# A radix-4 rewrite of the spectral layers of a four-layer mixer, with the layer norms regrouped

## The chip, the cores and the metric

The kernel runs on one core of one Trainium2 chip. The metric is the device time of one execution in microseconds; the kernel before takes 1835.26 us, the median of 4 runs.

## The reference, cut to what matters

The activations x are 2048 rows (S) of 512 columns (D). Two layer types alternate, A, B, A, B, each behind a layer norm without weights and added back to x. A is a spectral filter, a 2-D real FFT, a pointwise complex product with W, and the inverse; B is attention with 32 heads of 16 that share one key and one value head.

```python
def _A_ref(x, w_r, w_i):
    X = jnp.fft.rfft2(x.astype(jnp.float32), axes=(-2, -1))
    X = X * (w_r + 1j * w_i)
    return jnp.fft.irfft2(X, s=(S, D), axes=(-2, -1)).astype(jnp.bfloat16)
...
x = x + _A_ref(_layernorm(x), A_w_r, A_w_i)
x = x + _B_ref(_layernorm(x), B_wq, B_wk, B_wv, B_wo)
x = x + _A_ref(_layernorm(x), A_w_r, A_w_i)
x = x + _B_ref(_layernorm(x), B_wq, B_wk, B_wv, B_wo)
```

## The kernel before, in words

x stays in SBUF as `x_sb[p, r, t, d]`: row 512r + 4p + t, so 16 tiles of 128x512, named by r and t. `xn_sb` holds the normalised tiles in the same form.

**A spectral layer** (`spectral_layer`, `fft_layer`) has four stages, and every matmul in it has 128 rows of contraction.
- Stage A: all tiles are transposed on TensorE (L140), copied out (L146, L152, L154), and multiplied with the table PH of cosines and sines over D (L169); the result, a packed half of 256 real and 256 imaginary columns, is kept twice, as `Ppk` and with its halves swapped and one negated as `Psw` (L171 to L173).
- Stage B: for each t and each m (128 of the 512 frequencies k1), 8 matmuls over r with cosine and sine tables form a 512-point transform along S (L182, L184). ScalarE and VectorE turn the result by the twiddle factors, again into a plain and a swapped copy (L196 to L203). The four t are then combined by butterflies for k2 as matmuls with plus or minus identity (L220), each result of 128x512 is evacuated three times (L222 to L224), multiplied with W in 10 VectorE instructions (L228 to L236) and transformed back over k2 by identity matmuls and twiddles (L252 to L262).
- Stage C: the inverse 512-point transform along S (L277, 16 groups of 8 matmuls), its evacuation `AT` (L279), the inverse over D (L282 to L285) and the addition to x on VectorE (L297).
- The epilogue of each tile is the next layer's norm (`layernorm_tile`): statistics on VectorE (L108, L110), the square root on ScalarE (L112), reciprocal and a bias on VectorE (L113, L115), and the normalisation alternately on ScalarE (L121) and GpSimd (L118).

**An attention layer** starts with stage D: transposes of `xn_sb`, K and the first Q chunk, and V (L140, L342, L326, L355). Then `AttnLoop` writes its order out by hand, step by step: per step TensorE forms scores of two heads for ScalarE's exponential (L389, L500) and of one head for VectorE's (L504); VectorE and GpSimd make shifted copies of the latter (L462, L468); then come the products with V (L402). Every 11th step has no VectorE head and takes a piece from a list: a Q chunk (L326) or an output projection of a tile (`project`: L449, L451). In the first attention layer each projected tile goes on to the next spectral layer's norm (`layernorm_pool`): statistics on VectorE (L93, L95) and four GpSimd instructions (L97 to L102). After 22 steps `evacuate` copies the sums of 4 heads out (L411), and a chain over DRAM divides them. The last 4 projections of a layer come after its last step, when that chain has ended.

The rest of the program, the spectral layers and stage D among it, is put in order by a scheduler; on each engine that order then holds.

## Time and profile before

| | us |
|---|---|
| median of 4 runs (1834.03 to 1835.76) | 1835.26 |
| the profiled execution | 1834.03 |
| its span in the trace | 1831.5 |
| first spectral layer, stages A to C (from the start) | 172.1 |
| stage D and first attention loop with its division chain | 172.1 to 927.3 |
| last projections and second spectral layer | 927.3 to 1081.0 |
| stage D and second attention layer | 1081.0 to 1831.5 |

The 2.5 us between the execution's time and its span lie around the traced span. In the rows below a time is the start or duration of an instruction on the given engine; PE is TensorE's matmuls, DVE VectorE, ACT ScalarE, POOL GpSimd. The bracket at the end of a timeline row says how long the engine was idle ahead of it and what released it. In the rows of groups, the last numbers are busy time, mean duration in ns, and idle time ahead of the group with its releasers. Instructions on one engine overlap a little, so that starts lie closer than durations; a matmul's duration holds the time until its result has left the array.

### The profile page before, as it was taken

The numbers are of one execution on the slowest core, as the hardware profiler recorded it, in microseconds if no ns is written. First come the engines' busy times: TensorE is split into PE (matmuls) and PEld (weight loads), VectorE is DVE, ScalarE is ACT, GpSimd is POOL, SyncE is SP. The second block draws the span as 40 slices with busy tenths as digits, with TensorE's granted clock in tenths as the row PEclk, the third lists the DMA queues.
The fourth block names the chain that finished last, engine by engine and source line by source line (L and its number), as shares of the span: only waits on it lengthen the run. The fifth ranks groups of instructions, "written<-read, shape, count | busy, mean of one in ns | idle before, by whom it ended". The sixth has DMA issues, their size and how long they took to land.

```text
span 1831.5 us, 36065 instructions
## 1 busy us (share of the span) xinstructions
PE 1633.8 (89%) x13760; PEld 508.3 (28%) x13760; DVE 1567.6 (86%) x2919; ACT 1530.1 (84%) x1850; POOL 733.1 (40%) x744
## 2 busy tenths in 40 slices
PE   5878999998999899989868889999999999999995
PEld 2323322222222222222233342222222222222221
DVE  5776699999999999999848757999999999999995
ACT  6444699998999899999844447999999999999994
POOL 2001244456445644564410012444444454454443
PEclk9979899999999999999988898999999999999998
DMA  5000000000000000000000000000000000000000
GB/s 178 1 1 1 1 15 15 15 15 15 15 15 15 15 15 20 16 15 15 15 8 1 1 1 1 15 15 17 22 24 15 15 21 21 15 16 24 23 15 27
DMA packets 38733, 32.43 MB, mean 18 GB/s; under 512 B 21264, under 2 KB 28576, under 8 KB 38560
## 3 DMA queue, kind: packets, MB, share of 16 engines
q1 hardware_dynamic: 37600, 27.89, 5.1%
q8 instruction: 107, 1.75, 0.4%
q0 software_dynamic: 960, 2.25, 0.4%
q14 instruction: 66, 0.54, 0.1%
HBM read 24.88 MB, written 2.62 MB: 15 GB/s over the span
## 4 chain that ended last, share of the span: by engine, by line
PE 53%; DVE 30%; ACT 10%; issue 4%; DMA 2%; POOL 0%; SPq 0%; DVEq 0%; ACTq 0%; POOLq 0%
PE acc_new L402 21%; DVE t L504 13%; PE sd L389 13%; ACT e L500 8%; DVE tj L462 5%; PE sa L389 4%; PE ps L277 3%; DVE odd L437 2%; DVE on_new L434 2%; PE ps L169 2%; PE ps L326 2%; PE ps L449 2%; PE ps L184 2%; PE ps L182 2%; ACT den L411 1%
## 5 line engine op out<-in xcount | busy, mean ns | idle before, releaser
L500 ACT ACTIVATE e<-sa 128x1024 bf16<-128x1024 f32 x1408 | 1323.4, 1105 | 65.3 <-PE sa L389 61.9
L468 POOL TENSOR_SCALAR t<-tj 128x1024 int16<-128x1024 int16 x640 | 672.5, 1051 | 759.1 <-DVE tj L462 442.9
L504 DVE TENSOR_SCALAR t<-sd 128x512 int16<-128x512 f32 x1280 | 830.6, 681 | 76.2 <-PE sd L389 34.4
L389 PE MATMUL sa<-QT,KT 32*128 32x512 bf16 x2816 | 551.4, 385 | 12.1 <-ACT e L500 11.7
L389 PE MATMUL sd<-QT,KT 32*128 32x512 bf16 x1280 | 492.3, 385 | 76.6 <-DVE t L504 75.1
L402 PE MATMUL acc_new<-e,V 128*32 128x512 bf16 x2816 | 557.9, 393 | 1.0 <-ACT e L500 1.0
L462 DVE TENSOR_SCALAR tj<-t 128x2048 int16<-128x2048 int16 x640 | 443.0, 692 | 0.0
L402 PE MATMUL acc_new<-tj,V 128*32 128x512 bf16 x2560 | 386.8, 386 | 2.8 <-DVE tj L462 2.8
L402 PE MATMUL acc_new<-t,V 128*32 128x512 bf16 x2560 | 388.1, 387 | 1.0 <-POOL t L468 1.0
L389 PEld LDWEIGHTS <-KT 32*128 32x128 bf16 x4096 | 195.3, 91 | 690.5 <-issue 689.5
L402 PEld LDWEIGHTS <-V 128*32 128x32 bf16 x7936 | 159.3, 94 | 331.5 <-issue 331.1
L118 POOL TENSOR_SCALAR xn_sb<-x_sb,rstd,nb 128x512 bf16<-128x512 bf16 x16 | 12.2, 767 | 280.1 <-DVE mv L110 147.2
L449 PE MATMUL ps<-wo_sb,on_new 128*128 128x512 bf16 x128 | 36.3, 417 | 24.1 <-DMA on_new<-odd 24.1
L140 PE MATMUL ps<-tab_ident,xn_sb 128*128 128x128 bf16 x256 | 23.9, 248 | 33.2 <-ACT xn_sb L121 18.4
L222 ACT CAST Xs<-ps 128x512 bf16<-128x512 f32 x32 | 18.8, 588 | 37.9 <-DVE m L235 37.6
L297 DVE TENSOR_TENSOR x_sb<-ps,x_sb 128x512 bf16<-128x512 f32 x32 | 21.2, 674 | 32.8 <-PE ps L285 32.8
L437 DVE TENSOR_TENSOR odd<-den,rb 128x512 bf16<-128x512 f32 x32 | 37.5, 1173 | 13.0 <-DMA rb<-rd 12.8
L182 PE MATMUL ps<-Ppk,tab_C 128*128 128x512 bf16 x128 | 48.5, 379 | 0.0
L277 PE MATMUL ps<-tab_C,Dpk 128*128 128x512 bf16 x128 | 48.5, 379 | 0.0
L184 PE MATMUL ps<-Psw,tab_S 128*128 128x512 bf16 x128 | 48.5, 379 | 0.0
L112 ACT ACTIVATE rstd<-mv,eps 128x1 f32<-128x1 f32 x48 | 12.9, 288 | 40.8 <-DVE mv L110 38.2
L411 ACT COPY den<-acc_new 128x512 f32<-128x512 f32 x64 | 39.2, 612 | 8.8 <-PE acc_new L402 8.8
(100 smaller groups left out, 1037.3 us busy)
## 6 DMA issues: line engine op xcount, KB each, us to landing
rb<-rd SPq DMA_DIRECT2D x64, 256.0 KB
...
on_new<-odd SPq DMA_DIRECT2D x128, 16.0 KB
...
dq<-den SPq DMA_DIRECT2D x64, 8.0 KB
rd<-dq SPq DMA_DIRECT2D x64, 8.0 KB
...
```

The costliest lines, as they stand in the source:

```text
L182: nc.tensor.matmul(ps, lhsT=C512[:, r, m * P:(m + 1) * P], rhs=Ppk[:, rt, :], start=(k == 0), stop=False)
L184: nc.tensor.matmul(ps, lhsT=S512[:, r, m * P:(m + 1) * P], rhs=Psw[:, rt, :], start=False, stop=(r == R - 1))
L277: nc.tensor.matmul(ps, lhsT=lt, rhs=tab[:, m, :], start=(k == 0), stop=(k == 7))
L389: self.nc.tensor.matmul(out, lhsT=self.KT[32 * i:32 * i + 32, half, kc * P:(kc + 1) * P], rhs=self.QT[32 * i:32 * i + 32, g, qb * 512:(qb ...
L402: self.nc.tensor.matmul(self.acc[key][32 * i:32 * i + 32, :], lhsT=self.V4[:, kc, j, :], rhs=e, start=first, stop=False, skip_group_check= ...
L411: nc.scalar.copy(out=den, in_=self.acc.pop(key))
L437: nc.vector.tensor_tensor(out=odd, in0=den, in1=rb, op=ALU.mult)
L449: nc.tensor.matmul(ps, lhsT=on[:, g, qt * P:(qt + 1) * P], rhs=self.wo_sb[:, g, :], start=(g == 0), stop=(g == 3))
L462: nc.vector.tensor_scalar(out=tj, in0=cyc["t0"], scalar1=float(SH[j]), scalar2=None, op0=ALU.add)
L468: nc.gpsimd.tensor_scalar(out=cyc["t1"][:, h, :], in0=tj[:, h, :], scalar1=1.0, scalar2=float(SH[1] - SH[j]), op0=ALU.mult, op1=ALU.add)
L500: nc.scalar.activation(out=e, in_=sa, func=ACT.Exp, bias=EXP_LN, scale=SCALE)
L504: nc.vector.tensor_scalar(out=self.dcyc[c]["t0"][:, k, :], in0=sd, scalar1=Y_MUL, scalar2=Y_ADD, op0=ALU.mult, op1=ALU.add)
```

## The change

The spectral layer is rewritten; line numbers below are those of the changed kernel where the text says so.
- Over r, the 4-point butterflies now come first, on VectorE, as sums and differences of whole tiles (`ec`, `xc`, changed L159 to L162). Transposes and PH products keep their number (L169, L178), and 4 VectorE instructions and 3 ScalarE copies per t form `Y`.
- What is left of the transform along S has 128 points. Its twiddles are folded into a table `TAB` of 128 x 12288 (3 MB in all, where the dropped cosine and sine tables had 1.5 MB), and the sum over t runs inside one PSUM group: per (j2, k2) four matmuls of 512 columns (L205) and eight of 256 (L207, L209), where the swap of halves is made by writing to the other half of the bank.
- One evacuation per result (L211) in place of three; products with W and the back butterflies in all 18 VectorE instructions per j2 on 512 and 1024 columns (L214 to L226). There are no swapped copies and no twiddle instructions.
- The inverse along S takes 64 matmuls instead of 128 (L250), with windows of `TAB` as the moving operand, and a sum and a difference on VectorE (L255 to L257). x is added by a fifth matmul per output tile, with the identity (L260), and ScalarE writes the sum to `x_sb` (L266). The PSUM pool has 8 buffers instead of 4.
- The norm is one class for all layers: statistics per tile as before, the inverse root on GpSimd for four tiles at once (changed L105, L106), the normalisation on VectorE (L108) once all four r of a t are there. ScalarE's square root is gone. In the attention loop the four normalisations are put off by 4 to 7 steps.
- `x` is loaded in 4 pieces by t, `w_r` and `w_i` in 4 pieces each by j2; the attention loop's `t0` has 3 buffers.

The diff, cut to its core (shared helper functions and the removed bodies are left out):

```diff
@@ host_tables @@
+    tabs["TAB"] = bf(np.stack([np.sin(ang), np.cos(ang), -np.sin(ang), -np.cos(ang), np.sin(ang), np.cos(ang)], axis=3))
@@ layernorm @@
-def layernorm_pool(nc, lnpool, tabs, x_ap, xn_ap):
-def layernorm_tile(nc, lnpool, tabs, x_ap, xn_ap, on_act=True, use_pool=False):
...
+class LayerNorm:
...
+    def add(self, r, t, later=None):
+        nc = self.nc
...
+        stats = self.lnpool.tile([P, 6], F32, tag="ln_stats", bufs=4)
+        nc.vector.bn_stats(stats, self.x_sb[:, r, t, :])
+        nc.vector.bn_aggr(mv[:, r, :], stats)
+        self.n[t] += 1
+        if self.n[t] == R:
+            self.apply(t, self.mv.pop(t), later)
+    def apply(self, t, mv, later=None):
+        nc = self.nc
+        rstd = self.lnpool.tile([P, R], F32, tag="ln_rstd", bufs=3)
+        nc.gpsimd.tensor_tensor(out=rstd, in0=mv[:, :, 1], in1=self.tabs["eps"], op=ALU.add)
+        nc.gpsimd.tensor_tensor(out=rstd, in0=rstd, in1=self.tabs["mhalf"], op=ALU.pow)
+        def one(r):
+            nc.vector.tensor_scalar(out=self.xn_sb[:, r, t, :], in0=self.x_sb[:, r, t, :],
+                                    scalar1=mv[:, r, 0:1], scalar2=rstd[:, r:r + 1],
+                                    op0=ALU.subtract, op1=ALU.mult)
+        for r in range(R):
+            if later is None:
+                one(r)
+            else:
+                later(4 + r, lambda r=r: one(r))
@@ spectral layer @@
-def fft_layer(nc, tabs, work, psum, xT, wr_sb, win_sb, y_cb):
+def spectral_layer(nc, tc, tabs, x_sb, xn_sb, wr_sb, wi_sb, epilogue):
+    TAB, PH, PSC, PSS, ident = tabs["TAB"], tabs["PH"], tabs["PSC"], tabs["PSS"], tabs["ident"]
+    LO = slice(0, 256)
+    HI = slice(256, 512)
+    with tc.tile_pool(name="workA", bufs=2) as work, tc.tile_pool(name="psA", bufs=8, space=bass.MemoryType.PSUM) as psum:
+        Y = work.tile([P, T, 4, 512], BF, tag="big")
+        for t in range(T):
+            ec = work.tile([P, 2, 2, 512], BF, tag="ec")
+            xc = work.tile([P, 2, 512], BF, tag="xc")
+            nc.vector.tensor_tensor(out=ec[:, 0, :, :], in0=xn_sb[:, 0:2, t, :], in1=xn_sb[:, 2:4, t, :], op=ALU.add)
+            nc.vector.tensor_tensor(out=ec[:, 1, :, :], in0=xn_sb[:, 0:2, t, :], in1=xn_sb[:, 2:4, t, :], op=ALU.subtract)
+            nc.vector.tensor_tensor(out=xc[:, 0, :], in0=ec[:, 0, 0, :], in1=ec[:, 0, 1, :], op=ALU.add)
+            nc.vector.tensor_tensor(out=xc[:, 1, :], in0=ec[:, 0, 0, :], in1=ec[:, 0, 1, :], op=ALU.subtract)
+            xT = work.tile([P, 2, 2, NC, P], BF, tag="xTA")
+            banks = []
+            for pair, src in ((1, ec[:, 1, :, :]), (0, xc)):
+                ps = psum.tile([P, 2, NC, P], BF, tag="pa")
+                for q in range(2):
+                    for cc in range(NC):
+                        nc.tensor.transpose(ps[:, q, cc, :], src[:, q, cc * P:(cc + 1) * P], ident)
+                if pair == 0:
+                    nc.scalar.copy(out=xT[:, pair, :, :, :], in_=ps)
+                else:
+                    nc.vector.tensor_copy(out=xT[:, pair, :, :, :], in_=ps)
+            for pair in (1, 0):
+                for q in range(2):
+                    ps = psum.tile([P, 512], F32, tag="pa")
+                    for cc in range(NC):
+                        nc.tensor.matmul(ps, lhsT=xT[:, pair, q, cc, :], rhs=PH[:, cc, :],
+                                         start=(cc == 0), stop=(cc == NC - 1))
+                    banks.append(ps)
+            psC, psD, psP, psM = banks
+            dd = work.tile([P, 512], F32, tag="dd")
+            nc.scalar.copy(out=dd, in_=psD)
+            nc.vector.tensor_tensor(out=Y[:, t, 1, LO], in0=psC[:, LO], in1=dd[:, HI], op=ALU.subtract)
+            nc.vector.tensor_tensor(out=Y[:, t, 1, HI], in0=psC[:, HI], in1=dd[:, LO], op=ALU.add)
+            nc.vector.tensor_tensor(out=Y[:, t, 3, LO], in0=psC[:, LO], in1=dd[:, HI], op=ALU.add)
+            nc.vector.tensor_tensor(out=Y[:, t, 3, HI], in0=psC[:, HI], in1=dd[:, LO], op=ALU.subtract)
+            nc.scalar.copy(out=Y[:, t, 0, :], in_=psP)
+            nc.scalar.copy(out=Y[:, t, 2, :], in_=psM)
+        V = work.tile([P, T, 4, 512], BF, tag="big")
+        for j2 in range(4):
+            Xs = work.tile([P, 4, 512], BF, tag="Xs")
+            mr = work.tile([P, 4, 2, 256], BF, tag="mr")
+            mi = work.tile([P, 4, 2, 256], BF, tag="mi")
+            Z = work.tile([P, 4, 2, 256], BF, tag="Z")
+            ac = work.tile([P, 2, 2, 256], BF, tag="ac")
+            bd = work.tile([P, 2, 2, 256], BF, tag="bd")
+            Xv = Xs.rearrange("p k (h f) -> p k h f", h=2)
+            for q in range(2):
+                for k2 in (q, q + 2):
+                    ps = psum.tile([P, 512], F32, tag="pa")
+                    for t in range(T):
+                        n = (t * k2) % 4
+                        yt = Y[:, t, j2, :]
+                        nc.tensor.matmul(ps, lhsT=TAB[:, t, j2, (COS + n) % 4, :], rhs=yt, start=(t == 0), stop=False,
+                                         skip_group_check=True)
+                        nc.tensor.matmul(ps[:, LO], lhsT=TAB[:, t, j2, (SIN + n + 2) % 4, :], rhs=yt[:, HI],
+                                         start=False, stop=False, skip_group_check=True)
+                        nc.tensor.matmul(ps[:, HI], lhsT=TAB[:, t, j2, (SIN + n) % 4, :], rhs=yt[:, LO],
+                                         start=False, stop=(t == T - 1), skip_group_check=True)
+                    nc.scalar.copy(out=Xs[:, k2, :], in_=ps)
+                ks = slice(q, q + 3, 2)
+                for m_, w_ in ((mr, wr_sb), (mi, wi_sb)):
+                    nc.vector.tensor_tensor(out=m_[:, ks, :, :], in0=Xv[:, ks, :, :],
+                                            in1=w_[:, j2, ks, :].unsqueeze(2).to_broadcast([P, 2, 2, 256]),
+                                            op=ALU.mult)
+                nc.vector.tensor_tensor(out=Z[:, ks, 0, :], in0=mr[:, ks, 0, :], in1=mi[:, ks, 1, :], op=ALU.add)
+                nc.vector.tensor_tensor(out=Z[:, ks, 1, :], in0=mr[:, ks, 1, :], in1=mi[:, ks, 0, :], op=ALU.subtract)
+                nc.vector.tensor_tensor(out=ac[:, q, :, :], in0=Z[:, q, :, :], in1=Z[:, q + 2, :, :], op=ALU.add)
+                nc.vector.tensor_tensor(out=bd[:, q, :, :], in0=Z[:, q, :, :], in1=Z[:, q + 2, :, :], op=ALU.subtract)
+            Vv = V.rearrange("p t j (h f) -> p t j h f", h=2)
+            nc.vector.tensor_tensor(out=Vv[:, 0, j2, :, :], in0=ac[:, 0, :, :], in1=ac[:, 1, :, :], op=ALU.add)
+            nc.vector.tensor_tensor(out=Vv[:, 2, j2, :, :], in0=ac[:, 0, :, :], in1=ac[:, 1, :, :], op=ALU.subtract)
+            for tt, o0, o1 in ((1, ALU.add, ALU.subtract), (3, ALU.subtract, ALU.add)):
+                nc.vector.tensor_tensor(out=Vv[:, tt, j2, 0, :], in0=bd[:, 0, 0, :], in1=bd[:, 1, 1, :], op=o0)
+                nc.vector.tensor_tensor(out=Vv[:, tt, j2, 1, :], in0=bd[:, 0, 1, :], in1=bd[:, 1, 0, :], op=o1)
+        def window(j2, t, part):
+            tb = TAB[:, j2, t, :, :]
+            b0 = COS if part == 0 else SIN
+            if j2 == 2:
+                return tb[:, b0:b0 + 4, :]
+            w2 = tb[:, b0:b0 + 2, :]
+            if j2 == 0:
+                return w2.unsqueeze(1).to_broadcast([P, 2, 2, P])
+            step = {1: 1, 3: 3}[j2]
+            ap = bass.AP(tensor=w2.tensor, offset=w2.offset, ap=[w2.ap[0], [step * P, 2], [1, 2 * P]])
+            return ap
+        for t in range(T):
+            AT = work.tile([P, 2, 2, 512], BF, tag="AT")
+            for b in range(2):
+                banks = []
+                for js in ((0, 2), (1, 3)):
+                    ps = psum.tile([P, 512], F32, tag="pa")
+                    k = 0
+                    for j2 in js:
+                        for part in range(2):
+                            f0 = part * 256 + b * P
+                            nc.tensor.matmul(ps, lhsT=V[:, t, j2, f0:f0 + P], rhs=window(j2, t, part),
+                                             start=(k == 0), stop=(k == 3))
+                            k += 1
+                    banks.append(ps)
+                gh = work.tile([P, 512], F32, tag="dd")
+                nc.scalar.copy(out=gh, in_=banks[1])
+                nc.vector.tensor_tensor(out=AT[:, b, 0, :], in0=banks[0], in1=gh, op=ALU.add)
+                nc.vector.tensor_tensor(out=AT[:, b, 1, :], in0=banks[0], in1=gh, op=ALU.subtract)
+            for r in range(R):
+                ps = psum.tile([P, 512], F32, tag="pa")
+                nc.tensor.matmul(ps, lhsT=ident, rhs=x_sb[:, r, t, :], start=True, stop=False)
+                for b in range(2):
+                    for part, tab in ((0, PSC), (1, PSS)):
+                        f0 = ((r % 2) * 2 + part) * P
+                        nc.tensor.matmul(ps, lhsT=AT[:, b, r // 2, f0:f0 + P], rhs=tab[:, b, :],
+                                         start=False, stop=(b == 1 and part == 1))
+                nc.scalar.copy(out=x_sb[:, r, t, :], in_=ps)
+                epilogue(r, t)
@@ AttnLoop @@
-        self.epilogue(r, t)
+        self.epilogue(r, t, self.at)
...
-                t0 = self.expp.tile([P, 4, 512], I16, tag="t0")
+                t0 = self.expp.tile([P, 4, 512], I16, tag="t0", bufs=3)
```

How the rows stand on an engine, before and after, at three places. First VectorE in the middle of stage B. Before, these are the rows of one product tile (m_752, m_753 and m_759 are scratch buffers, `win_sb` is the negated imaginary part of W):

```order
L228 TENSOR_TENSOR m_752<-Xs,wr_sb 128x256 [waits DVE_49,Activation_49]
L229 TENSOR_TENSOR m_753<-Xs,win_sb 128x256 [waits Activation_49]
L228 TENSOR_TENSOR m_752<-Xs,wr_sb 128x256
L229 TENSOR_TENSOR m_753<-Xs,win_sb 128x256 [waits Activation_49]
L230 TENSOR_TENSOR Zpk<-m_752,m_753 128x512 [waits DVE_49]
```

After, the second half of one j2, with the butterflies that follow it:

```order
L214 TENSOR_TENSOR mr<-Xs,wr_sb 128x2x512 [waits Activation_49]
L214 TENSOR_TENSOR mi<-Xs,wi_sb 128x2x512
L217 TENSOR_TENSOR Z<-mr,mi 128x2x256 [waits DVE_49]
L218 TENSOR_TENSOR Z<-mr,mi 128x2x256
L219 TENSOR_TENSOR ac<-Z 128x512 [waits DVE_49]
L220 TENSOR_TENSOR bd<-Z 128x512
L222 TENSOR_TENSOR V<-ac 128x512 [waits DVE_49]
L223 TENSOR_TENSOR V<-ac 128x512
L225 TENSOR_TENSOR V<-bd 128x256 [waits DVE_49]
L226 TENSOR_TENSOR V<-bd 128x256
```

Before, 5 rows made half of one tile's product (5 more make the swapped half); after, six rows make the product and the first back butterfly of two tiles, and six per j2 (the last two not shown) the second butterfly.

Second, TensorE at the same place. Before, butterfly matmuls of 512 columns with the identity, or its negative `nident`, as weights:

```order
L220 LDWEIGHTS tab_ident [waits DVE_49]
L220 MATMUL ps<-Bpk,tab_ident 128x512 [waits Activation_49]
L220 LDWEIGHTS tab_ident
L220 MATMUL ps<-Bsw,tab_ident 128x512
L220 LDWEIGHTS tab_nident [waits DMAHW3_49]
L220 MATMUL ps<-Bpk,tab_nident 128x512
```

After, the first rows of the first (j2, k2) group, with a part of `TAB` as weights:

```order
L205 LDWEIGHTS tab_TAB [waits DMAHW6_49]
L205 MATMUL ps<-Y,tab_TAB 128x512 [waits PE_49]
L207 LDWEIGHTS tab_TAB
L207 MATMUL ps<-Y,tab_TAB 128x256
L209 LDWEIGHTS tab_TAB
L209 MATMUL ps<-Y,tab_TAB 128x256
L205 LDWEIGHTS tab_TAB
L205 MATMUL ps<-Y,tab_TAB 128x512
```

Twelve such matmuls make one group; nothing on TensorE waits for VectorE between the groups but for free buffers.

Third, VectorE in stage C. Before, the additions to x and the norm's small steps, in the order of the tiles:

```order
L297 TENSOR_TENSOR x_sb<-ps,x_sb 128x512 [waits PE_49] x2
L108 BN_STATS stats<-x_sb 128x6 [waits DVE_49] x2
L110 BN_AGGR mv<-stats 128x2 [waits DVE_49]
L297 TENSOR_TENSOR x_sb<-ps,x_sb 128x512 [waits PE_49]
L113 RECIPROCAL rstd<-rstd 128x1 [waits Activation_49]
```

After, between the outputs of t = 0 and those of t = 1:

```order
L96 BN_STATS stats<-x_sb 128x6 [waits Activation_49]
L97 BN_AGGR mv<-stats 128x2 [waits DVE_49] x2
L256 TENSOR_TENSOR AT<-ps,gh 128x512 [waits Activation_49]
L108 TENSOR_SCALAR xn_sb<-x_sb,mv,rstd 128x512 [waits Pool_49]
L108 TENSOR_SCALAR xn_sb<-x_sb,mv,rstd 128x512
L108 TENSOR_SCALAR xn_sb<-x_sb,mv,rstd 128x512 [waits DVE_49] x2
L257 TENSOR_TENSOR AT<-ps,gh 128x512
```

`AT`, which TensorE needs for the next outputs, now stands on VectorE behind a normalisation that waits for GpSimd.

261 lines of the change are left out of this document (43 added, 218 removed).

## The prediction

> **What bounds the kernel now.** I read the windows of the stages first. The time, 1831.5 us of span, is two spectral layers and two attention layers one behind the other; the windows show the spectral ones (columns: us, then busy us and instructions of PE, PEld, DVE, ACT, POOL, the granted clock, the DMA share, GB/s).
>
> ```profile
> span 1831.5 us, 36065 instructions
> ...
> 0.00:29.70 29.70, 8.34 (x60) 5.54 (x61) 17.89 (x72) 16.03 (x33) 9.42 (x16) 1.00 0.92 273
> 29.70:44.80 15.10, 15.10 (x69) 6.89 (x68) 7.94 (x18) 12.80 (x30) 0.00 (x0) 1.00 0.01 2
> 44.80:72.40 27.60, 27.60 (x129) 12.50 (x128) 17.09 (x49) 12.33 (x23) 0.00 (x0) 1.00 0.00 1
> 72.40:130.30 57.90, 40.69 (x130) 14.14 (x129) 52.02 (x187) 27.99 (x64) 0.00 (x0) 0.73 0.00 1
> 130.30:172.10 41.80, 41.80 (x194) 18.57 (x193) 22.90 (x69) 15.92 (x34) 6.11 (x8) 1.00 0.00 1
> 172.10:199.70 27.60, 18.62 (x177) 10.35 (x177) 12.20 (x31) 12.82 (x20) 0.00 (x0) 0.88 0.01 1
> ...
> 938.20:954.70 16.50, 16.50 (x67) 7.00 (x65) 6.37 (x15) 13.33 (x31) 0.00 (x0) 0.83 0.01 1
> 954.70:982.30 27.60, 27.60 (x129) 12.50 (x128) 17.25 (x48) 12.14 (x22) 0.00 (x0) 1.00 0.00 1
> 982.30:1039.70 57.40, 40.65 (x131) 14.11 (x129) 51.66 (x186) 27.84 (x64) 0.00 (x0) 0.73 0.00 1
> 1039.70:1081.00 41.30, 41.30 (x192) 18.41 (x191) 23.09 (x70) 17.13 (x35) 6.07 (x8) 1.00 0.00 0
> ```
>
> Stage A ends at 44.8 and 954.7, stage B at 130.3 and 1039.7, stage C at 172.1 and 1081.0. In the first third of B (44.8 to 72.4) and in all of C, TensorE is never idle: a matmul of 512 columns takes 27.60 / 129 = 0.214 us. In the 57.9 us between, VectorE is busy for 52.0. The timeline there shows the loop, here ScalarE's row of one tile and two of VectorE's, then two waits of this window (us in total, times, longest):
>
> ```profile
> 86.02 0.58 ACT L222 CAST Xs<-ps 128x512 bf16<-128x512 f32 x1 [1.72 <-DVE m L235]
> 88.86 0.59 ACT L222 CAST Xs<-ps 128x512 bf16<-128x512 f32 x1 [1.71 <-DVE m L235]
> ```
> ```profile
> 87.86 0.29 DVE L234 TENSOR_TENSOR m<-Xs,wr_sb 128x256 bf16<-128x256 bf16 x1
> 88.07 0.28 DVE L235 TENSOR_TENSOR m<-Xs,win_sb 128x256 bf16<-128x256 bf16 x1
> ```
> ```profile
> ACT Xs L222 <- DVE m L235: 18.7, 11, 1.8
> PE ps L220 <- ACT Xs L224: 11.2, 10, 1.9
> ```
>
> A tile takes 2.84 us, ScalarE waits for VectorE's products, TensorE for ScalarE: VectorE sets the end, and its rows start 0.08 us closer than they last. Nothing else runs beside a spectral layer, so what it loses in time the kernel loses.
>
> **Stage B.** Prices from the groups (last numbers: busy us, mean ns, idle):
>
> ```profile
> L234 DVE TENSOR_TENSOR m<-Xs,wr_sb 128x256 bf16<-128x256 bf16 x64 | 18.4, 287 | 1.0
> L230 DVE TENSOR_TENSOR Zpk<-m,m 128x512 bf16<-128x512 bf16 x32 | 13.6, 424 | 1.2
> L222 ACT CAST Xs<-ps 128x512 bf16<-128x512 f32 x32 | 18.8, 588 | 37.9 <-DVE m L235 37.6
> L297 DVE TENSOR_TENSOR x_sb<-ps,x_sb 128x512 bf16<-128x512 f32 x32 | 21.2, 674 | 32.8 <-PE ps L285 32.8
> L173 DVE CAST Psw<-ps 128x256 bf16<-128x256 f32 x32 | 13.6, 424 | 18.4 <-ACT Psw L172 18.4
> ```
>
> All matmuls, evacuations and products of the old B go: 85.5 us in the first layer, 85.0 in the second. New on TensorE: 16 groups of 4 x 0.214 and 8 x 0.107 us (half the columns) = 1.71, 27.4 in all. New on VectorE per half of a j2: two products of 1024 columns and four instructions of 512. From 256 to 512 columns the price grows by 0.137 us, so 1024 cost 0.424 + 2 x 0.137 = 0.70; 2 x 0.70 + 4 x 0.42 = 3.08, less three overlaps of 0.08 = 2.84. The second butterfly adds 2 x 0.424 + 4 x 0.287 - 5 x 0.08 = 1.59. Four j2: 4 x (2 x 2.84 + 1.59) = 29.1. ScalarE copies 16 times 0.588, well hidden. The first product waits for two groups and a copy, 3.4 + 0.2 + 0.59 = 4.2; so B lasts 33.3, say 33.5. **Saved: 52.0 and 51.5 us.** TensorE and VectorE are nearly even; VectorE ends last. That products with W, repeated over the halves by a zero step, run as fast as plain ones no row shows: at one column a cycle (674 - 424 = 250 ns for 256 columns of PSUM source, so 0.674 + 0.50 = 1.17) each costs 0.47 more. I take 0.70, the row with the same types.
>
> **Stage C.** The old one is 192 matmuls, TensorE without a gap. New: 64 + 80 = 144, 30.8 us. Of them 12 with early j2 and 4 with the identity can run while VectorE finishes B (TensorE is done after 27.4 of 33.5): -3.4. Against that stand waits for `AT`: at the first t four instructions of 0.674 behind the last V, some 3 us; later VectorE is held up by the norm standing ahead of `AT`, of which GpSimd's part is
>
> ```profile
> L98 POOL TENSOR_TENSOR rstd<-rstd,mhalf 128x1 f32<-128x1 f32 x16 | 8.8, 551 | 1.3
> L110 DVE BATCH_NORM_AGGREGATE mv<-stats 128x2 f32<-128x6 f32 x48 | 7.8, 166 | 0.0
> L108 DVE BATCH_NORM_STATS2 stats<-x_sb 128x6 f32<-128x512 bf16 x48 | 31.4, 675 | 10.5 <-DMA x_sb<-in_A_x_dram 10.5
> ```
>
> less than a us per t behind the matmuls of the next t, 1.4 for three. C lasts 31.8, so **10.0 and 9.5 us saved**. If `AT` came 3 us late at every t, C would be 37.
>
> The normalisation itself, 512 columns with two scalars read per partition, VectorE does nowhere yet. Neighbours:
>
> ```profile
> L565 DVE TENSOR_SCALAR win_sb<-win_sb 128x4096 bf16<-128x4096 bf16 x1 | 1.2, 1227 | 0.4 <-DMA win_sb<-in_A_w_i_dram 0.4
> L462 DVE TENSOR_SCALAR tj<-t 128x2048 int16<-128x2048 int16 x640 | 443.0, 692 | 0.0
> L504 DVE TENSOR_SCALAR t<-sd 128x512 int16<-128x512 f32 x1280 | 830.6, 681 | 76.2 <-PE sd L389 34.4 <-PE sa L389 10.9
> ```
>
> L565 against L462 gives 0.261 ns a column, so 0.692 - 1536 x 0.261 = 0.29 us; L504, from PSUM, gives 0.68. I take 0.29, since source, type and engine are those of the first two. The Trainium skill, page "VectorE: DVE Perf Modes", section "The perf-mode tier table (the rule you actually need)", lets such an instruction on bf16 in SBUF run at four columns a cycle and one on two tensors at two; by it both choices made here hold, at 0.68 the sum would be about 22 us smaller.
>
> **Stage A.** First layer: x lands in four pieces. The whole took
>
> ```profile
> 0.73 10.60 DMA x_sb<-in_A_x_dram
> ```
>
> so I put the first piece at 5 us (bounds 3.4, a quarter, and 12.5, all together). VectorE's 16 statistics at 0.675 + 0.166 - 0.10 take 11.9, to 16.9. Twelve normalisations at 0.21 and four aggregations bring 19.7, a difference, four more normalisations and a second one 21.9, transposes and a copy 23.5. Then each t needs 16 transposes and 16 matmuls:
>
> ```profile
> 187.20 0.61 PE L140 MATMUL ps<-tab_ident,xn_sb 128*128 128x128 bf16 x8 [0.34 <-DVE KT L348]
> ```
>
> Eight in 0.61 with a tail of about 0.16, 0.06 each; 0.9 + 3.4 + 0.4 for VectorE's copy = 4.7, four t 18.8, end 42.3 instead of 44.8: **2.5 saved**. In VectorE's order all statistics stand ahead of the first normalisation, so a late piece delays everything by as much, 7.5 at the bound. The tables grow by 1.6 MB: 29.7 us x 273 GB/s = 8.1 MB become 9.7, ended at 35.5 us at that rate, while `TAB` is first used at 42.3; hidden, with 7 us to spare.
>
> Second layer: it starts with the last projections:
>
> ```profile
> 927.34 4.26 PE L449 MATMUL ps<-wo_sb,on_new 128*128 128x512 bf16 x13 [11.19 <-DMA on_new<-odd]
> ```
>
> All its matmuls stand behind these on TensorE. On VectorE three additions with statistics, 1.5 us each, and two differences come first, so that PH starts near 937.4 (938.2 before), but then transposes, differences and PH of four t follow, 18.8: 956.2 against 954.7, **1.5 lost**.
>
> **Stage D.** Unchanged matmuls; `AT` and the norm hold the first K groups up:
>
> ```profile
> 178.33 3.57 PE L342 MATMUL ps<-xT,wka 128*128 128x512 bf16 x8 [2.71 <-DVE nb L115]
> 188.59 1.90 PE L342 MATMUL ps<-xT,wka 128*128 128x512 bf16 x8 [0.79 <-DVE xT L146]
> ```
>
> K began 6.2 us after C. Now copy, statistics, a GpSimd step of 0.55 and a smaller one, four normalisations and a transpose copy stand there, 4.7; **1.5 saved** in each layer. No square root means no table switch of ScalarE; in C it was hidden.
>
> **Attention.** The sums of four heads are copied out here, in the first layer with two normed tiles between the copies, in the second with two stored ones:
>
> ```profile
> 405.16 0.61 ACT L411 COPY den<-acc_new 128x512 f32<-128x512 f32 x1
> 429.81 0.61 ACT L411 COPY den<-acc_new 128x512 f32<-128x512 f32 x1
> ...
> 1314.18 0.61 ACT L411 COPY den<-acc_new 128x512 f32<-128x512 f32 x1
> 1336.41 0.61 ACT L411 COPY den<-acc_new 128x512 f32<-128x512 f32 x1
> ```
>
> 24.65 against 22.23: a norm costs 1.2 us a tile, 0.84 of it statistics that stay. Twelve tiles can give back 12 x 0.36 = 4.3 from GpSimd and pay 12 x 0.29 = 3.5 to VectorE, or 8.2 at 0.68. I take 0, bounds -4.3 and +8.2. The third buffer of `t0` counts 0: L504's waits above are for scores of its own step, not for a buffer.
>
> **The sum.** First layer 2.5 + 52.0 + 10.0 + 1.5 = 66.0, second -1.5 + 51.5 + 9.5 + 1.5 = 61.0, together 127.0. The profiled execution took 1834.03; 1834.0 - 127.0 = 1707.0. It is 1.2 below the median of 1835.26, so the forecast is 1708.
>
> **The rivals.**
> - *VectorE at one column a cycle.* Products: 16 x 0.47 x 2 = 15, 1723. Normalisations at 0.68: 12 us in the first layer's chain (32 x 0.39), 6 in the second, 5 in attention, 1731; both 1746. The type of the operands speaks against; that no row has these forms speaks for. 0.20.
> - *Loads.* Pieces of x or `TAB` late by 8 us: 1716. A DMA share of 0.92 until 29.7 speaks for it. 0.05.
> - *The throttle, slower than before.* The window at 72.4 had a granted clock of 0.73 with waits of at most 1.9 us, and the first K group ran at 0.45 us a matmul, double. The spectral matmuls of a layer are 17.3 + 27.4 + 30.8 = 75.5 us; all at half, TensorE sets A to C at 151 and some 9 of waits, 76 more than 84: 2 x 76 - 127 = +25, 1860. It decides against the kernel once more than 127 / 151, 84% of that work, runs at half. Dense windows at 1.00 and a TensorE busy nine tenths speak against. 0.03. The Trainium skill, "TensorE: Matmul & The Clock Gate", section "What's actually happening", halves the clock after an idle window of about 3.4 us; by that no stage here would fall and 1708 holds, but the 1.9 us above show that shorter waits do it.
> - *Nothing saved*, because attention or a chain around it takes back the time: no view shows work beside the spectral layers. 0.01, 1835.
>
> **How the numbers follow.** The forecast has 0.71, with 1690 to 1722 as its own range (norms giving back 4, B and C as even as TensorE alone; or `AT` late at each t, 5 a layer, and slow stretches of clock). Up to 1738 come late loads and most of a slow VectorE. Over by 0.2%, about what a measurement of this kernel can tell from no change, is faster in all but the last two: 0.96, same 0.01, slower 0.03.
>
> **What would show it.** Right: B of 33 to 34 us with TensorE gapless for its first 27, products near 0.70, normalisations near 0.29, C near 32, PE clock 1.00 there, copies L411 24 to 25 us apart where norms stand. Wrong: products above 1.1, B above 40, matmuls of 0.43 spacing in B or C, a TensorE that waits for `TAB`, attention steps longer by more than 8 us in sum.

## The result and the profile after

The changed kernel takes 1691.82 us, the median of 8 runs (1690.46 to 1694.26), against 1834.54 for the kernel before, run beside it (13 runs). The ratio is 0.9223, with a 95% interval of 0.9213 to 0.9233. That is 142.7 us less; the forecast of 1708 had 127 less. The profiled execution is the slowest of the eight, 1694.26 us with a span of 1692.4, 139.1 below the span of before.

The windows of the changed kernel by stage, with the columns of the prediction (us, then busy us and instructions of PE, PEld, DVE, ACT, POOL, the granted clock, DMA share, GB/s):

```profile
0.00:24.60 24.60, 0.00 (x1) 0.01 (x1) 17.43 (x53) 1.28 (x1) 14.60 (x24) 1.00 0.96 312
24.60:45.45 20.85, 19.83 (x129) 10.82 (x129) 14.02 (x33) 10.49 (x15) 0.00 (x0) 1.00 0.37 94
45.45:73.20 27.75, 27.75 (x193) 18.75 (x192) 22.97 (x59) 9.37 (x16) 0.00 (x0) 1.00 0.00 1
73.20:110.00 36.80, 32.01 (x146) 13.75 (x145) 29.52 (x73) 13.37 (x24) 3.62 (x6) 1.00 0.00 1
110.00:137.15 27.15, 19.07 (x177) 10.81 (x176) 11.22 (x22) 8.35 (x12) 1.21 (x2) 0.87 0.00 1
137.15:843.40 706.25, 663.98 (x6116) 186.79 (x6113) 654.81 (x1086) 672.53 (x735) 340.29 (x326) 0.99 0.05 15
843.40:857.37 13.97, 0.81 (x6) 0.28 (x4) 0.94 (x2) 0.58 (x1) 0.00 (x0) 0.65 0.08 25
857.37:866.90 9.53, 6.77 (x30) 3.30 (x31) 8.31 (x17) 0.00 (x0) 0.49 (x2) 0.68 0.00 0
866.90:886.20 19.30, 17.75 (x112) 9.06 (x113) 13.81 (x34) 10.49 (x15) 0.71 (x1) 0.97 0.00 1
886.20:914.00 27.80, 27.80 (x194) 18.79 (x193) 23.03 (x59) 9.36 (x16) 0.00 (x0) 1.00 0.00 1
914.00:950.90 36.90, 32.09 (x146) 13.72 (x144) 29.62 (x73) 13.37 (x24) 3.62 (x6) 1.00 0.00 0
950.90:977.80 26.90, 18.60 (x177) 10.44 (x177) 11.08 (x22) 8.35 (x12) 1.20 (x2) 0.94 0.01 2
977.80:1670.90 693.10, 661.80 (x6116) 185.45 (x6115) 639.52 (x1050) 670.80 (x736) 338.05 (x326) 0.99 0.06 18
1670.90:1692.40 21.50, 5.36 (x15) 1.56 (x13) 3.71 (x6) 0.00 (x0) 1.13 (x2) 0.58 0.12 40
```

Stage B is the third row and the tenth, TensorE's 16 groups without a gap at a clock of 1.00; the rows behind them are C. The prediction showed no windows of the attention loops before; they are:

```profile
199.70:913.50 713.80, 661.05 (x6115) 185.59 (x6112) 663.65 (x1074) 673.37 (x735) 364.94 (x368) 0.99 0.05 15
913.50:927.34 13.84, 2.65 (x37) 2.18 (x36) 0.95 (x2) 0.58 (x1) 0.00 (x0) 0.73 0.09 26
1108.70:1809.00 700.30, 659.52 (x6113) 183.87 (x6112) 650.48 (x1050) 670.58 (x736) 338.52 (x326) 0.99 0.06 17
1809.00:1831.50 22.50, 6.11 (x16) 1.89 (x14) 3.71 (x6) 0.49 (x1) 1.13 (x2) 0.69 0.12 39
```

Subtracting stage by stage gives where the 139.1 us come from, beside what the sum had for each:

| stage | saved, measured | saved, forecast |
|---|---|---|
| A, first layer (44.8, now 45.45) | -0.65 | 2.5 |
| B and C, first layer (127.3, now 64.55) | 62.75 | 62.0 |
| D, first layer (27.6, now 27.15) | 0.45 | 1.5 |
| first attention loop (713.8, now 706.25) | 7.55 | 0 |
| its end, to the last projections (13.84, now 13.97) | -0.13 | 0 |
| A, second layer (27.36, now 28.83) | -1.47 | -1.5 |
| B and C, second layer (126.3, now 64.7) | 61.6 | 61.0 |
| D, second layer (27.7, now 26.9) | 0.8 | 1.5 |
| second attention loop and its end (722.8, now 714.6) | 8.2 | 0 |

The rewrite of B and C came out as forecast within 1.4 us in 123. Two things did not: the attention loops are 15.75 us shorter, which the sum had at 0, and the places where the norm stands on the path gave 1.25 - 0.65 = 0.6 where the sum had 5.5.

The groups of the changed kernel with the prices that the prediction had to bound:

```profile
L214 DVE TENSOR_TENSOR mr<-Xs,wr_sb 128x1024 bf16<-128x1024 bf16 x16 | 11.0, 686 | 8.7 <-ACT Xs L211 8.7
L108 DVE TENSOR_SCALAR xn_sb<-x_sb,mv,rstd 128x512 bf16<-128x512 bf16 x64 | 23.3, 418 | 11.0 <-POOL rstd L106 11.0
L106 POOL TENSOR_TENSOR rstd<-rstd,mhalf 128x4 f32<-128x4 f32 x16 | 17.6, 1113 | 1.0
L105 POOL TENSOR_TENSOR rstd<-mv,eps 128x4 f32<-128x4 f32 x16 | 3.4, 218 | 198.7 <-DVE mv L97 198.6
```

The product with a repeated W takes 0.686 us (0.70 forecast, 1.17 for the rival). The normalisation takes 0.418, between the two bounds of 0.29 and 0.68. GpSimd's power on four columns takes 1.113, twice the 0.551 of one column; with the addition ahead of it (0.218) that is 1.33, where the sum had a step of 0.55 and "a smaller one".

### The profile page after: what moved, and what is told of

Read it like the earlier page. It is cut to its first block, busy times and chain, and to the rows that moved or that the text cites. A ratio compares the mean times of both kernels' runs of the same rounds, so it can differ in the third digit from the quotient of the medians.

```text
span 1692.4 us, 34864 instructions
## 1 busy us (share of the span) xinstructions
PE 1533.6 (91%) x13536; PEld 483.5 (29%) x13536; DVE 1480.0 (87%) x2582; ACT 1428.3 (84%) x1607; POOL 704.9 (42%) x696
## 4 chain that ended last, share of the span: by engine, by line
PE 54%; DVE 27%; ACT 11%; issue 4%; DMA 2%; POOL 1%; SPq 0%; ACTq 0%; DVEq 0%; POOLq 0%
PE acc_new L369 25%; PE sd L356 15%; DVE t L471 10%; ACT e L467 9%; PE sa L356 5%; DVE tj L429 4%; DVE odd L404 2%; DVE on_new L401 2%; DVE stats L96 2%; PE ps L416 2%; PE ps L293 2%; ACT den L378 1%; PE ps L178 1%; DVE xn_sb L108 1%; PE ps L309 1%
## 5 line engine op out<-in xcount | busy, mean ns | idle before, releaser
L471 DVE TENSOR_SCALAR t<-sd 128x512 int16<-128x512 f32 x1280 | 829.5, 677 | 70.6 <-PE sd L356 60.3
L429 DVE TENSOR_SCALAR tj<-t 128x2048 int16<-128x2048 int16 x640 | 436.0, 682 | 0.0
L105 POOL TENSOR_TENSOR rstd<-mv,eps 128x4 f32<-128x4 f32 x16 | 3.4, 218 | 198.7 <-DVE mv L97 198.6
L96 DVE BATCH_NORM_STATS2 stats<-x_sb 128x6 f32<-128x512 bf16 x64 | 42.4, 678 | 12.4 <-ACT x_sb L266 6.7
L171 ACT COPY xT<-ps 128x1024 bf16<-128x1024 bf16 x8 | 8.1, 1012 | 50.2 <-PE ps L169 50.2
L211 ACT CAST Xs<-ps 128x512 bf16<-128x512 f32 x32 | 18.7, 585 | 36.8 <-PE ps L209 36.8
L205 PE MATMUL ps<-Y,tab_TAB 128*128 128x512 bf16 x128 | 48.5, 379 | 0.0
L401 DVE TENSOR_TENSOR on_new<-den,rb 128x512 bf16<-128x512 f32 x32 | 39.9, 1247 | 1.4 <-DMA rb<-rd 1.4
L266 ACT CAST x_sb<-ps 128x512 bf16<-128x512 f32 x32 | 17.6, 589 | 25.9 <-PE ps L264 25.9
```

Of the source, the lines that this page charges most:

```text
L96: nc.vector.bn_stats(stats, self.x_sb[:, r, t, :])
L205: nc.tensor.matmul(ps, lhsT=TAB[:, t, j2, (COS + n) % 4, :], rhs=yt, start=(t == 0), stop=False, skip_group_check=True)
L401: nc.vector.tensor_tensor(out=on[:, g, :], in0=den, in1=rb, op=ALU.mult)
L429: nc.vector.tensor_scalar(out=tj, in0=cyc["t0"], scalar1=float(SH[j]), scalar2=None, op0=ALU.add)
L471: nc.vector.tensor_scalar(out=self.dcyc[c]["t0"][:, k, :], in0=sd, scalar1=Y_MUL, scalar2=Y_ADD, op0=ALU.mult, op1=ALU.add)
```

## The experiments

The runs came in three groups, each beside runs of the kernel before, whose median was 1834.06, 1831.02 and 1831.36 us. The changed kernel itself was not repeated in them, so ratios to the kernel before are compared with its 0.9223 (0.9213 to 0.9233), and stage times with its trace.

| run | median us | ratio to before (95%) |
|---|---|---|
| t0, two buffers | 1710.50 | 0.9330 (0.9316 to 0.9344) |
| kernel before, t0 three buffers | 1817.83 | 0.9917 (0.9901 to 0.9934) |
| no power | 1683.47 | 0.9183 (0.9166 to 0.9199) |
| AT first | 1692.01 | 0.9229 (0.9216 to 0.9243) |
| one product | 1689.70 | 0.9224 (0.9205 to 0.9243) |
| three products | 1700.17 | 0.9288 (0.9267 to 0.9309) |
| x in one transfer | 1698.47 | 0.9274 (0.9252 to 0.9295) |
| first norm by t | 1690.40 | 0.9228 (0.9210 to 0.9247) |
| old norm | 1680.67 | 0.9173 (0.9154 to 0.9192) |
| root on ScalarE | 1682.84 | 0.9182 (0.9163 to 0.9201) |
| root on ScalarE, norm by t | 1678.18 | 0.9163 (0.9145 to 0.9182) |
| constants in the norm (one run, no interval) | 1675.01 | |

Stage times of the profiled executions, for what follows: the start of stage B of the first layer, and the time from the start of B to the first K matmul (B, C and the first norm of D) in each layer. Where a run leaves stage A as it is, B starts between 44.19 (t0 with two buffers) and 45.45. The spread lies in the loads: the second piece of x keeps VectorE waiting for 1.79 us in the changed kernel's trace, for 0.35 in that with two buffers, and not at all in those with the old norm or the root on ScalarE. The changed kernel's wait is the longest of these, so up to 1.8 us of a gain in that column can be spread.

| run | B starts | B to K, first | B to K, second |
|---|---|---|---|
| the changed kernel | 45.45 | 70.78 | 70.69 |
| no power | 43.15 | 67.06 | 66.90 |
| AT first | 44.83 | 69.80 | 69.70 |
| one product | 44.87 | 69.84 | 69.75 |
| three products | 44.33 | 76.40 | 75.89 |
| x in one transfer | 52.51 | 70.81 | 70.72 |
| first norm by t | 42.11 | 70.80 | 70.72 |
| old norm | 40.24 | 65.67 | 65.69 |
| root on ScalarE | 43.26 | 66.91 | 66.78 |
| root on ScalarE, norm by t | 39.75 | 66.92 | 66.80 |

**The third buffer of t0, both ways.** In the changed kernel:

```diff
-                t0 = self.expp.tile([P, 4, 512], I16, tag="t0", bufs=3)
+                t0 = self.expp.tile([P, 4, 512], I16, tag="t0")
```

> The changed kernel, but with two buffers of t0 in the attention loop, as before the change. Theory (the third buffer is worth the missing time: with two, the first L471 of every four waits for VectorE's own shift L429, which has just started, to end): the evacuations without extra work stand 21.30 us apart again instead of 21.10, those with a piece of extra work 0.33 longer, so 7 to 8 us more in each attention layer, 1691.8 + 15 = 1707. Rival (the attention layers are shorter for another reason, GpSimd's lighter norm or the new layout of the buffers): spacing stays 21.10, time 1692.

The reverse edit alone in the kernel before:

> The kernel before, with three buffers of t0 and nothing else changed. Theory (own-engine wait): spacing 21.10, 1834.5 - 15 = 1819.5, whatever the spectral layers are. Rival (another reason, which came with the rewritten layers or the new norm): 1834.5 and spacing 21.30.

Measured: 18.7 us more for the changed kernel, 16.2 less for the kernel before. ScalarE's copies of the sums show it in the intervals without extra work. First the changed kernel, then it with two buffers, then the kernel before with three:

```profile
298.82 0.61 ACT L378 COPY den<-acc_new 128x512 f32<-128x512 f32 x1
319.92 0.61 ACT L378 COPY den<-acc_new 128x512 f32<-128x512 f32 x1
```
```profile
276.62 0.61 ACT L378 COPY den<-acc_new 128x512 f32<-128x512 f32 x1
297.93 0.61 ACT L378 COPY den<-acc_new 128x512 f32<-128x512 f32 x1
```
```profile
359.43 0.61 ACT L411 COPY den<-acc_new 128x512 f32<-128x512 f32 x1
380.55 0.61 ACT L411 COPY den<-acc_new 128x512 f32<-128x512 f32 x1
```

21.10, 21.31 and 21.12 us apart; it was 21.30 before. The reason is visible on VectorE. In the timeline of the kernel before, a shift (tj) is followed by the first two heads of the next four:

```profile
344.75 0.68 DVE L462 TENSOR_SCALAR tj<-t 128x2048 int16<-128x2048 int16 x1
345.54 1.29 DVE L504 TENSOR_SCALAR t<-sd 128x512 int16<-128x512 f32 x2
```

and in the changed kernel:

```profile
281.20 0.68 DVE L429 TENSOR_SCALAR tj<-t 128x2048 int16<-128x2048 int16 x1
281.80 1.32 DVE L471 TENSOR_SCALAR t<-sd 128x512 int16<-128x512 f32 x2
```

With two buffers the head writes the buffer that this very shift reads, so it waits for VectorE itself, and starts 0.79 us behind the shift; with three, 0.60. In the order of the instructions it is a plain entry, first of before, then of the changed kernel:

```
L504 TENSOR_SCALAR t_2258<-sd 128x512 [waits DVE_49,PE_49]
L504 TENSOR_SCALAR t_2258<-sd 128x512 [waits PE_49]
```
```
L471 TENSOR_SCALAR t_1660<-sd 128x512 [waits PE_49] x2
```

So 0.19 us stood once per four heads, 5 times in 22 steps; of these 0.95 us, 0.2 show in a plain interval and 0.33 in one with extra work, the rest lies in time in which VectorE waits for scores. The theory holds. The groups of the two kernels with three buffers, the changed one first, show the same from another side:

```profile
L471 DVE TENSOR_SCALAR t<-sd 128x512 int16<-128x512 f32 x1280 | 829.5, 677 | 70.6 <-PE sd L356 60.3 <-PE sa L356 10.1
```
```profile
L504 DVE TENSOR_SCALAR t<-sd 128x512 int16<-128x512 f32 x1280 | 830.7, 679 | 65.7 <-PE sd L389 62.0 <-PE sa L389 3.7
```

Nearly all idle time has a releaser there, 70.4 of 70.6 us and 65.7 of 65.7. In the row of the kernel before, which the prediction shows, 34.4 + 10.9 of 76.2 us have one; with two buffers in the changed kernel it is 42.5 of 73.3. The Trainium skill, "VectorE: DVE Perf Modes", section "The DRAIN you can't avoid", says that a semaphore between two VectorE instructions costs nothing, since the next one waits for the pipe to empty anyway; by that the third buffer would be worth 0. The trace disagrees by 0.19 us for each such wait, and the two runs by 16 and 19 us.

**The norm's GpSimd step.** The power is left out:

```diff
-        nc.gpsimd.tensor_tensor(out=rstd, in0=rstd, in1=self.tabs["mhalf"], op=ALU.pow)
```

> The changed kernel without GpSimd's inverse root (it leaves out the power; the factor is variance plus eps). It takes away 1.113 us from every chain of a norm, and nothing else. Theory (the norm's GpSimd step is on the path: VectorE stood 11.0 us ahead of its normalisations, TensorE 3.7 us per layer for AT and 4.4 for the first K group): up to 1.1 us once in the first stage A and four times in each spectral layer from stage C on, 1 + 2 x 4.4 = 10, so 1682. Rival (those waits only cover work of VectorE or TensorE that is late anyway): at most 2 us, 1690.

Measured: 8.35 us less (1683.47), B starts 2.3 us earlier in the trace, and B to K is 3.7 and 3.8 shorter. The theory holds. Where the power delays the kernel can be read in the waits of the changed kernel (us in all, times, longest), ahead of the same waits for `AT` without the power:

```profile
DVE xn_sb L108 <- POOL rstd L106: 11.0, 10, 1.4
PE ps L309 <- DVE xT L136: 13.4, 8, 4.4
PE ps L264 <- DVE AT L256: 5.3, 4, 1.3
PE ps L264 <- DVE AT L257: 2.2, 2, 1.1
```
```profile
PE ps L263 <- DVE AT L255: 1.6, 4, 0.5
...
PE ps L263 <- DVE AT L256: 0.3, 2, 0.2
```

VectorE waits up to 1.4 us ahead of a t's four normalisations, in stage C with `AT` queued behind them; TensorE, in turn, waits for `AT` up to 1.3 us, 7.5 in both layers, and for the first K group 4.4. Without the power the 7.5 are 1.9.

**AT ahead of the normalisations.**

```diff
+            for fn in held:
+                fn()
+            held = []
             for r in range(R):
...
-                epilogue(r, t)
+                epilogue(r, t, lambda d, fn: held.append(fn))
```

> The changed kernel with the normalisations of a t, in stage C, put off until AT of the next t has been issued; the count of instructions is the same. Theory (AT stands behind a normalisation that waits for GpSimd): of TensorE's 3.7 us of waits for AT in each layer two thirds or all go, 2 x 2.5 to 2 x 3.7 us, 1684.5 to 1687. Rival (AT is late by its own chain: the matmuls L250, ScalarE's copy, two instructions of 0.68): the waits stay and the time is 1691 to 1692.

Measured: 1692.01, no change. The edit did what it says only for the first t: behind the other two the scheduler put three of the four normalisations ahead of `AT` again, and they still waited 1.40 us for GpSimd. TensorE's waits for `AT` fell from 3.72 to 2.26 us in the first layer, and B to K by 1.0 in both. In the profiled execution 1.9 of these 2 us were lost again in one attention interval, of 23.95 us at a granted clock of 0.93 against 22.09 us at 1.00 in the changed kernel.

For the time this run is inconclusive: 2 us are less than the width of the interval of its ratio.

**One product and three.** Does VectorE set the end of B, as the sum had it? One run leaves half the products out, one makes half of them twice:

```diff
-                for m_, w_ in ((mr, wr_sb), (mi, wi_sb)):
+                for m_, w_ in ((mr, wr_sb),):
...
+                nc.vector.tensor_tensor(out=mx[:, ks, :, :], in0=Xv[:, ks, :, :], in1=w_b, op=ALU.mult)
```

(w_b stands for the broadcast part of `wr_sb`; the first two lines belong to the one run, the last to the other.)

> The changed kernel without the products with the imaginary part of W (the sums take the real product twice): 8 instructions of 1024 columns less on VectorE in each spectral layer, 0.60 us apart, so 4.8 us of VectorE's work in stage B; TensorE's matmuls are as before. Theory (TensorE and VectorE are so even that TensorE sets the end as soon as VectorE is a little earlier; TensorE waited only 0.83 and 0.24 us at the seam of B and C): 1.1 us per layer less and the other 3.7 hidden, 1690. Rival (VectorE alone sets the end of B, as the prediction's sum has it): 3 to 4.8 us per layer less, 1682 to 1686.

> The changed kernel with the product with the real part of W made a second time into a scratch tile that nothing reads: 8 more instructions of 1024 columns on VectorE in each spectral layer, 4.8 us of its work. Theory (VectorE is already the later of the two by about 1 us at the seam of B and C, so work added to it shows in full, while work taken from it hardly did): 4.8 us later at the seam in each layer, 1692 + 9.6 = 1701. Rival (VectorE has room beside TensorE, whose 16 groups and early matmuls of C fill the stage): at most 1 to 2 us per layer, 1693 to 1696.

Measured: with 4.8 us less of VectorE's work a layer, 0.94 us less from B to K, and 1689.70, which is no difference by the ratio; with 4.8 more, 5.6 and 5.2 us, 1700.17. With one product the theory holds: the two engines were even to within a us. With three the time is the theory's 1701, but its mechanism is only part of it. TensorE at the seam of B and C, in the changed kernel and then with three products (L254 and L264 there are L250 and L260):

```profile
73.23 2.75 PE L250 MATMUL ps<-tab_TAB,V 128*128 128x512 bf16 x12
75.83 1.03 PE L260 MATMUL ps<-x_sb,tab_ident 128*128 128x512 bf16 x4
77.68 1.04 PE L250 MATMUL ps<-tab_TAB,V 128*128 128x512 bf16 x4 [0.83 <-DVE V L222]
78.96 1.02 PE L250 MATMUL ps<-tab_TAB,V 128*128 128x512 bf16 x4 [0.24 <-ACT gh L255]
```
```profile
74.71 1.03 PE L264 MATMUL ps<-x_sb,tab_ident 128*128 128x512 bf16 x4
79.67 3.59 PE L254 MATMUL ps<-tab_TAB,V 128*128 128x512 bf16 x8 [3.94 <-DVE V L226]
```

The 12 matmuls with early j2 and the 4 with the identity fill the time that VectorE is behind, as the prediction had it, and 0.83 + 0.24 us of waiting are left. VectorE's last piece of V, in the same two runs:

```profile
78.48 0.28 DVE L226 TENSOR_TENSOR V<-bd 128x256 bf16<-128x256 bf16 x1
```
```profile
80.48 0.28 DVE L230 TENSOR_TENSOR V<-bd 128x256 bf16<-128x256 bf16 x1
```

From the start of B (45.45 and 44.33) its end is 33.31 and 36.43 us away, so of 4.8 us of added work 3.1 show on VectorE, in the second layer too. A wait of 0.59 us for `Xs` is gone, and the third product fills the 0.12 us that a sum had waited for the product just ahead of it, 8 times. The other 2.5 us of the first layer's 5.6, and 2.1 of the second's 5.2, come after that, on TensorE: behind its wait of 3.94 us the next matmuls start 0.43 apart in place of 0.215.

**x in one transfer.** Four transfers by t become one of the whole `x_sb`.

> The changed kernel with x loaded by one transfer instead of four by t. In the kernel before, the whole landed 10.60 us after its issue, against 4.3 us for the first statistics here. Theory (all statistics stand ahead of the first normalisation, and 11.9 us of them follow the first piece, so that a later start shifts the chain): statistics begin near 11.4 and end near 23.3 instead of 16.6, stage B starts 6 to 7 us later, 1698. Rival (the pieces share the queues and the second is what holds the chain, so splitting brought little): 0 to 3 us, 1692 to 1695.

Measured: B starts 7.06 us later (up to 8.3 against the earliest start with four pieces), and the time is 1698.47. The theory holds. VectorE's chain of the changed kernel, from the first piece on, and then the first statistics of this run:

```profile
4.30 1.29 DVE L96 BATCH_NORM_STATS2 stats<-x_sb 128x6 f32<-128x512 bf16 x2 [3.41 <-DMA x_sb<-in_A_x_dram]
...
11.41 0.69 DVE L96 BATCH_NORM_STATS2 stats<-x_sb 128x6 f32<-128x512 bf16 x1 [1.79 <-DMA x_sb<-in_A_x_dram]
...
16.57 3.95 DVE L108 TENSOR_SCALAR xn_sb<-x_sb,mv,rstd 128x512 bf16<-128x512 bf16 x12
...
22.56 1.38 DVE L108 TENSOR_SCALAR xn_sb<-x_sb,mv,rstd 128x512 bf16<-128x512 bf16 x4 [1.18 <-POOL rstd L106]
```
```profile
11.62 1.29 DVE L96 BATCH_NORM_STATS2 stats<-x_sb 128x6 f32<-128x512 bf16 x2 [10.72 <-DMA x_sb<-in_A_x_dram]
```

**The first norm by t.** The loop over all 16 tiles ahead of the layers is gone, and the loop over t of the first stage A begins with the four tiles of its t:

```diff
+            for r in range(R if first else 0):
+                first(r, t)
             ec = work.tile([P, 2, 2, 512], BF, tag="ec")
```

> The changed kernel with the first norm written inside the loop over t of the first stage A; the same instructions, but on VectorE only 5 normalisations, not 16, stand ahead of the first butterfly. Theory (the first transposes at 24.6 wait for normalisations that the first t does not need, and TensorE sets the pace from there): first transposes some 4 us earlier, stage B starts 3 to 4 us earlier than 45.4, 1688 to 1689. Rival (VectorE is busy through all of stage A, so the order changes nothing at its end): 1691 to 1692.

Measured: B starts 3.34 us earlier in the trace, as the theory has it, though part of it can be spread; the time of 1690.40 is 0.9228 of before, no difference that the runs can tell. By the trace VectorE was not busy through A; whether the 3.3 us reach the end, this run alone leaves open.

**The norm of before in the changed kernel.** The class's statistics and normalisation are replaced by calls of the old functions, `layernorm_pool` in the attention loop and `layernorm_tile` elsewhere:

> The changed kernel with the norm of before: per tile, the root on ScalarE, the normalisation on ScalarE and GpSimd (in the attention loop all of it on GpSimd). Theory (the new norm is the part that lost against the sum: GpSimd's 1.1 us and normalisations of 0.42 instead of 0.29 on VectorE, which is busy in A and C): the old one is no worse, stage B starts 2 to 5 us earlier, the waits for AT shrink, attention about the same: 1682 to 1692. Rival (the prediction's terms for A and D: new norm ahead by 2.5 - 1.5 + 2 x 1.5): 1695 to 1698.

Measured: 1680.67, ratio 0.9173: the new norm costs 9 to 11 us against the old one. B starts 5.2 us earlier, at least 3.4 of them not spread, and B to K is 5.1 and 5.0 shorter. So the regrouped norms take back part of what the rest of the change gains.

**The root on ScalarE, and both edits.**

```diff
-        nc.gpsimd.tensor_tensor(out=rstd, in0=mv[:, :, 1], in1=self.tabs["eps"], op=ALU.add)
-        nc.gpsimd.tensor_tensor(out=rstd, in0=rstd, in1=self.tabs["mhalf"], op=ALU.pow)
+        if later is None:
+            nc.scalar.activation(out=rstd, in_=mv[:, :, 1], func=ACT.Sqrt, bias=self.tabs["eps"][:, 0:1], scale=1.0)
+            nc.vector.reciprocal(rstd, rstd)
+        else:
+            nc.gpsimd.tensor_tensor(out=rstd, in0=mv[:, :, 1], in1=self.tabs["eps"], op=ALU.add)
+            nc.gpsimd.tensor_tensor(out=rstd, in0=rstd, in1=self.tabs["mhalf"], op=ALU.pow)
```

> The changed kernel with the inverse root for the first norm and in the spectral layers as a square root of four columns on ScalarE and a reciprocal on VectorE; GpSimd keeps it in the attention loop. Theory (GpSimd's 0.22 + 1.11 on the path): about 0.3 + 0.2 in their place, so half to two thirds of what leaving the power out gave (8.4): 1686 to 1688. Rival (the change of ScalarE's table to the exponential comes back on the path, 1.3 us ahead of each attention layer, and ScalarE's queue delays the root behind copies): 1690 to 1694.

With the first norm by t as well:

> The changed kernel with the root on ScalarE (as in the run with the square root) and the first norm written inside the loop over t (as in that run). Theory (the two act in different places, stage A of the first layer and every chain of a norm): their gains add, 9 + 3 = 12 less than 1692, 1679 to 1681. Rival (with the shorter root the first stage A is already bound by VectorE's own work): no better than the root alone, 1683.

Measured: 1682.84 with the root alone (0.9182 of 1834.5 is 1684.5), 1.5 to 3 us below the range of its theory; 1678.18 with both. From B to K the root alone gains 3.9 us in each layer, as much as leaving the power out (3.7 and 3.8), though two steps take its place here; why, no run shows. In the trace the gains at the start of B add, as far as the spread lets one tell: 2.2 and 3.3 apart, 5.7 together. The two new steps, in the groups of the run with both edits:

```profile
L106 ACT ACTIVATE rstd<-mv,eps 128x4 f32<-128x4 f32 x12 | 3.6, 298 | 12.7 <-DVE mv L97 12.5
L107 DVE RECIPROCAL rstd<-rstd 128x4 f32<-128x4 f32 x12 | 1.9, 162 | 2.0 <-ACT rstd L106 2.0
```

0.298 + 0.162 = 0.46 us in the place of 1.33. This version keeps every other part of the change and is faster than both kernels: 0.9163 (0.9145 to 0.9182) against 0.9223 (0.9213 to 0.9233), two intervals that do not touch.

**Constants in the norm.**

```diff
-                                    scalar1=mv[:, r, 0:1], scalar2=rstd[:, r:r + 1],
+                                    scalar1=0.01, scalar2=1.01,
```

> The changed kernel with two constants in the place of the mean and the factor in the normalisation (it leaves out the use of the statistics, so the wait for GpSimd goes too). Theory (the two scalars read per partition set the price of 0.418 us): with constants the same instruction takes 0.29, as the shift of 2048 columns implies. Rival (its two operations, or the bf16 arithmetic, set it): 0.42 again. In time, either way, about what the wait for GpSimd and the norm's place on the path are worth: 1676 to 1686.

Measured, in the groups of this run:

```profile
L108 DVE TENSOR_SCALAR xn_sb<-x_sb 128x512 bf16<-128x512 bf16 x64 | 18.0, 302 | 0.0
```

0.302 against 0.418 with the two scalars read per partition; the two operations are the same. The theory holds for the price; the one time, 1675.01, lies 1 us below its range.

## Why the prediction was right, and which of its terms were off

- **What bounds it, and stage B.** Right. Nothing runs beside the spectral layers, and what they lost came off the time: 124.35 us in B and C of both layers, 123.0 forecast. The product's price, the copy's place and the near evenness of TensorE and VectorE were as worked out. That VectorE ends last is right by about 1 us only: less work of it hardly shows, and of 4.8 us more 3.1 show on VectorE itself.
- **Stage C.** Right in the sum, with its parts shifted, so that the sum is in part luck. Of the 64.55 us of B and C TensorE is busy for 27.75 + 32.01 = 59.76 and waits 4.79: 1.07 at the seam, where some 6 were forecast, and 3.72 for `AT` at the later t, where it was 1.4. The run without the power shows GpSimd as the cause of most of the latter: both layers' 7.5 us become 1.9.
- **Stage A.** In the second layer right to 0.03 us. In the first, mis-sized by 3.15 (by 1.9 in the trace whose B starts earliest): the statistics end at 16.65, where 16.9 was forecast, which is luck, since they took 0.66 us a tile instead of 0.74 but waited 1.79 for the second piece; 12 normalisations then take 3.95 us instead of 2.5, and the last four wait 1.18 for GpSimd, which the working left out. First PH at 26.47 instead of 23.5; from there the 18.8 forecast became 19.0.
- **Stage D.** Mis-sized by 1.75 in both layers together, by the same two prices, 1.33 for GpSimd's steps and 0.418 for a normalisation; without the power the first K group's longest wait is 3.4 us in place of 4.4.
- **The normalisation's price.** The choice of 0.29, taken from rows whose scalars are constants, failed: with constants it is 0.302, with scalars per partition 0.418. The table of the Trainium skill that the prediction weighed ("VectorE: DVE Perf Modes", "The perf-mode tier table (the rule you actually need)") has one entry for both; the trace parts them, and its 0.418 decides.
- **Attention.** The norms there cost what the sum had, nothing: the four intervals that one t's norms stretch went from 24.65 + 24.52 + 2 x 22.22 = 93.61 to 23.47 + 24.59 + 22.09 + 21.89 = 92.04 us, 1.57 less, of which 4 x 0.33 come from the buffer as in the second layer; in the kernel before with three buffers the four take 92.18 us, 0.14 from the 92.04. The third buffer of t0 was put at 0, and this is the term that failed: 16 to 19 us. The prediction argued from the releasers named for L504, "for scores of its own step, not for a buffer". But that row gives 34.4 + 10.9 us of releasers for 76.2 us of idle time; 30.9 had none, against 0.2 of 70.6 us with three buffers. A wait of VectorE for itself is not in that list. The order of the instructions has it, as shown above, and the timeline as a step of 0.79 in place of 0.60.
- **The rivals.** No product at one column a cycle, while a normalisation went a third of the way from 0.29 to 0.68; the loads cost a wait of 1.79 us for the second piece; the throttle stayed away, 1.00 in B and C of both layers. That the total lies in the forecast's own range, 1.8 us above its low end, is luck: about 16 us gained in a term that was put at 0 stand against 5 lost in the norm's terms, and without that loss it would be near 1687. What the range's low end was argued from, norms that give back 4 us and a B and C as even as TensorE alone, is not what brought it there. With two buffers of `t0` the time is 1710.50, 2.5 us from the forecast of 1708.
